# A cross network in one-and-a-half levels of Winograd products: two tiles side by side, a third inner product, residual sums by DMA

## The chip, the cores and the metric

The kernel runs on one core of a Trainium2 chip. A core has five engines, each with an instruction queue that it works off in order: TensorE (PE) multiplies, VectorE (DVE) and ScalarE (ACT) work elementwise, GpSimd (POOL) and SyncE (SP) here mostly issue transfers. They wait for each other by semaphores. Operands lie in SBUF, 128 partitions wide; products land in PSUM, eight banks of 128 x 512 float32. Sixteen DMA engines move data between HBM and SBUF.

The metric is the device time of one execution in microseconds, the median over runs.

## The reference

A deep cross network with L = 6 layers on B = 16384 tokens of D = 1024 features, in bfloat16:

```
x = x0
for l in range(6):
    proj = einsum('bd,de->be', x, ws[l]) + bs[l]     # 16384 x 1024 times 1024 x 1024
    x = x0 * proj + x
return x
```

The work is six 1024 x 1024 matrix products for every token, and beside each a bias, a product with `x0` and a residual sum.

## The kernel before, in words

**Tiles.** Activations are held transposed: features on partitions, tokens along the free dimension. A tile (`pair`, `pr`) has 1024 tokens; there are 16. A *unit* is one layer of one tile; there are 96, in the order tile 0 layers 0 to 5, tile 1 layers 0 to 5, and so on (`units`). `x0T` holds the tile's input, `xst` its running x, each in two buffers that the tiles take in turn; each is cut in four blocks by feature half and token half: B11, B12, B21, B22 (`blk`).

**Seven products instead of eight.** A unit is a 2 x 2 block product by Winograd's variant of Strassen's method. Four sums of input blocks (T1 to T4, VectorE) and four sums of weight blocks (named 5, 6, 7, 3) allow seven block products: P1, P2, P5, P6, P3, P7, P4. Each is 512 x 512 weights on 512 tokens: four groups (`group`, line 286) of four matmuls of 512 columns, every group into one PSUM bank. The groups of P1, P6, P7 and P4 go into banks `pA`, those of P2, P5, P3 into banks `pX`. ScalarE empties the banks: `biased` (line 296) adds the layer's bias and writes one of the SBUF tiles `ev` (P1s, P5s, Q, U, V, W), `copy` (line 293) copies without bias, F.m from `pA` to `pX` so that P3 accumulates on P6's partial sum. VectorE then adds P5's part (Ua, Va) and P1's (Q1), multiplies by `x0` (Qm, Um, Vm, Wma, Wmb) and adds the old x (Qa, Ux, Vx, Wx). All these elementwise operations go through `tt` (line 202).

**A second level inside two products.** In most units products 5 and 2 are themselves split into seven (`inner`, line 398): 28 matmuls of 256 columns in place of 16 of 512. That needs three more VectorE operations ahead (t13, t2, t4), seven copies on ScalarE (e_p5, f1, e_c11, f2, e_c12, e_u3, e_c21) and one more sum on VectorE (cc) for each such product, and inner weight sums (5i, 2i). The first tile's six units and the last unit are one-level (`level1`): there 112 matmuls of 512 columns; elsewhere 80 of 512 and 56 of 256.

**Weights.** The first tile's units load the raw weight blocks, make the sums 5, 6, 7, 3 and the inner sums on VectorE (`combo`, `icombo`) and save these to HBM (`Lc`, `save`, line 306, issued by GpSimd). Later units load everything, nine tiles of 512 KB, into a ring of 16 (`ring_seq`, `pump`, line 250, SP's queue). A tile is reloaded as soon as its last use has been emitted.

**Order of the work.** Every operation carries a rank, written by hand or found before and kept as text (`R2`, `R0`, `EARLY`, `RLAST`): a time within its unit. A heap emits the operations whose predecessors are emitted in the order of unit start plus rank; each engine's queue has the order that results. On SP's queue weight loads stand between the transposing loads of the next tile's `x0` (`ld`, line 533), the transposes of finished tiles (`tro`, line 538) and their stores (`sto`, line 544).

**The last unit** is one-level and has its own end: its parts are transposed by DMA and on TensorE and stored in pieces.

Of the kernel before, what the change touches and what calls it, by code (L numbers as in the profile page):

```python
# [16 lines left out]

def ranks(text):

    return {w.split("@")[0]: float(w.split("@")[1]) for w in text.split()}  # L20

R2 = ranks("""
P1.0@0 P1.2@0.86 5p5@1.73 5p1@2.16 P1.3@2.6 2p1@3.46 5p2@3.9 5p6@4.34 2p5@4.78 P1.1@5.21 5p7@6.08 5p3@6.51 2p2@6.95
2p6@7.39 5p4@7.82 P6.0@8.26 P6.1@9.13 2p7@9.99 2p3@10.43 P3.0@10.86 2p4@11.73 P6.2@12.16 P6.3@13.03 P3.1@13.89
P3.2@14.75 P3.3@15.62 P7.1@16.48 P7.0@17.34 P7.2@18.21 P7.3@19.07 P4.1@19.93 P4.0@20.8 P4.2@21.66 P4.3@22.52
E1.0@1.07 5e_p5@2.38 5f1@3.03 E1.2@3.48 5e_c11@4.55 5f2@5.2 2e_p5@5.65 2f1@6.3 5e_u3@6.75 E1.3@7.23 2e_c11@7.8 E1.1@8.28  # L30
2f2@8.85 5e_c21@9.33 F.0@9.81 5e_c12@10.43 2e_u3@10.9 2e_c12@11.38 F.1@11.86 2e_c21@12.37 E3.0@12.85
F.2@13.45 F.3@14.1 E3.1@14.96 E3.2@15.82 E3.3@16.69 E7.0@18.41 E7.1@18.98 E7.2@19.55 E7.3@20.14 E4.0@21.87 E4.1@22.44
E4.2@23.01 E4.3@23.59
T1@-1.14 5t13@0.59 5t2@3.06 2t13@3.39 5t4@5.13 2t2@6.6 T2@6.93 2t4@8.07 T4@8.4 T3@9.6 5cc@10.88 2cc@12.61 Q1@13.35
Qm@14.62 Qa@15.89 Ua@17.43 Um@18.7 Ux@19.97 Va@21.11 Wma@23.38 Wmb@24.58 Wx@25.31 Vm@27.38 Vx@28.85
""")
R0 = ranks("""
P1.0@0 P1.1@.9 P1.2@1.7 P1.3@2.6 P2.2@3.5 P2.3@4.4 P2.1@5.2 P2.0@6.1 P5.2@6.9 P5.1@7.8 P5.0@8.7 P5.3@9.5
P6.2@10.4 P6.0@11.3 P6.1@12.1 P6.3@13 P7.2@13.9 P3.2@14.7 P7.1@15.6 P3.1@16.4 P3.0@17.3 P7.0@18.2 P3.3@19 P7.3@19.9
P4.0@20.8 P4.2@21.6 P4.1@22.5 P4.3@23.3  # L40
F1.2@2.8 F1.0@3.2 F1.3@3.7 F1.1@4.1 E2.2@4.6 E2.1@6.3 E2.0@7.2 E2.3@7.7 E5.2@8.3 F.2@11.5 E5.1@11.9 E5.3@12.4
F.1@13.2 E5.0@13.6 E7.2@14.9 E3.2@15.8 F.0@16.4 E7.1@16.8 F.3@17.4 E3.1@17.8 E7.0@19.2 E3.0@19.8 E3.3@20.4
E7.3@21 E4.0@21.8 E4.2@22.7 E4.1@23.6 E4.3@24.4
Qm@14.5 Qa@18.6 Ua@21.1 Um@22.4 Va@23.5 Wma@25.2 Wmb@25.3 Wx@26.4 Ux@27.6 T1@4.6 Vm@30 Vx@31.2 T2@8.3 T3@9.8 T4@13
c5@-8.6 c6@-6.8 c7@-4.5 c3@11.9 2i7@-7.4 2i5@-7.1 2i6@.5 2i3@9.4 5i5@10.9 5i7@11.2 5i6@11.6 5i3@14.2
""")
SAVES = ranks("gate@15 s5@16 s6@17 s7@18 s3@20 s2i@21 s5i@22")
EARLY = [ranks("""
t0.0@-4.00 u0.0@-3.70 t0.1@-3.80 u0.1@-3.50 t0.2@-3.60 u0.2@-3.30 t0.3@-3.40 u0.3@-3.10
t1.0@-1.90 u1.0@-1.60 t1.1@-1.70 u1.1@-1.40 t1.2@-1.50 u1.2@-1.20 t1.3@-1.30 u1.3@-1.00  # L50
t2.0@.3 t2.1@.4 t2.2@2.1 t2.3@2.2 u2.0@.5 u2.1@.6 u2.2@2.2 u2.3@2.3
P1.1@-2.83 bT@-2.4 P1.0@-1.96 P1.2@-1.10 P1.3@-.24 P2.1@1.27 P2.0@3.3 P2.2@4.49 P2.3@5.35 P5.1@6.94 P5.0@7.81 P5.3@8.67
P5.2@9.53 P6.3@10.52 P6.2@11.38 P6.0@12.24 P7.3@13.11 P6.1@13.97 P7.0@14.83 P4.3@15.70 P7.2@16.56 P7.1@17.42
P4.0@18.29 P4.2@19.15 P4.1@20.01 P3.0@20.88 P3.1@21.74 P3.3@22.60 P3.2@23.47
F1.1@-.9 F1.0@-.8 F1.2@2.25 F1.3@2.35 E2.1@2.7 E2.0@4.60 E2.2@5.56 E2.3@6.42 E5.3@9.74 E5.0@10.22 F.3@11.59
E5.2@12.07 E5.1@12.54 F.0@13.31 E7.3@14.18 F.2@14.75 F.1@15.23 E7.0@15.90 E4.3@16.77 E7.2@17.63 E7.1@18.49 E4.2@20.22
E4.0@20.79 E4.1@21.36 E3.0@21.95 E3.1@22.81 E3.3@23.67 E3.2@24.54
T1@3.57 c5@5.67 c5b@5.8 c6@5.9 T2@9.25 2i5@9.3 2i7@9.4 2i6@9.5 c7@10.38 T3@11.52 T4@12.65 2i3@13.79 c3@14.12
Qm@15.26 5i5@17.53 Va@19.74 Qa@20.88 Vm@22.01 Wma@23.15 Wmb@23.75 Wx@24.49 Ua@25.63 Um@26.90 Ux@28.17 5i7@29.30
Vx@30.77 5i6@31.91 5i3@41.53  # L60
"""), ranks("""
P1.3@.13 P1.2@.99 P1.0@1.86 P1.1@2.72 P2.2@3.58 P2.3@4.45 P2.0@5.31 P2.1@6.17 P5.3@7.04 P5.2@7.90 P5.1@8.76 P5.0@9.62
P6.3@10.49 P6.1@11.35 P6.2@12.21 P7.3@13.08 P6.0@13.94 P7.2@14.80 P4.3@15.67 P7.0@16.53 P7.1@17.39 P4.2@18.26
P3.3@19.12 P4.0@19.98 P4.1@20.85 P3.0@21.71 P3.1@22.57 P3.2@23.44
F1.2@2.06 F1.3@2.54 F1.0@3.02 F1.1@3.79 E2.3@5.52 E2.2@6.09 E2.1@7.24 E2.0@7.81 E5.3@8.38 E5.1@9.83 F.3@11.56
E5.2@12.04 F.1@12.51 E5.0@12.99 F.2@13.47 E7.3@14.15 F.0@15.01 E7.2@15.87 E7.0@17.60 E7.1@18.46 E4.3@19.03 E4.2@19.61
E3.3@20.19 E4.1@21.92 E4.0@22.49 E3.0@23.06 E3.1@23.64 E3.2@24.51
c5@-7.81 2i5@-5.93 c6@-5.59 T1@5.44 5i5@8.04 T2@8.38 2i6@9.51 c7@9.85 2i3@10.98 T3@11.32 5i6@12.45 T4@12.79 c3@13.92
Qm@15.06 2i7@17.00 Qa@17.67 Va@19.21 Wmb@20.35 Vm@20.95 Wma@23.23 Wx@23.97 Ua@25.25 5i7@26.39 Um@26.72 Ux@27.99
Vx@30.40 5i3@33.80  # L70
"""), ranks("""
# [77 lines left out]
def kernel(  # L149
# [13 lines left out]
    H = D // 2  # L163
    NB = 512
    PR = 2 * NB
    assert D == 1024 and B % PR == 0
    NPAIR = B // PR
    KQ, HQ, NQ = KH // 2, H // 2, NB // 2
    RING = 16
# [475 lines left out]
```

## Time and profile before

| | us |
|---|---|
| median of 3 runs | 2270.79 (2270.66 to 2271.06) |
| profiled execution, span | 2269.4 |
| TensorE busy | 2248.5 |
| VectorE busy | 2092.1 |
| ScalarE busy | 1847.8 |
| GpSimd busy | 24.5 |
| a steady two-level unit | 23.38 |

| DMA | |
|---|---|
| moved | 557.02 MB, mean 245 GB/s |
| SP's queue, share of 16 engines' time | 78.6% |
| GpSimd's queue | 2.3% |
| landing of a weight tile of 512 KB, median | 4.7 us (saved sums), 5.2 us (raw weights) |
| landing of a transpose, median | 7.3 us |
| landing of an output store of 1 MB, median | 8.8 us |

The profiled execution's own time is the span from its first to its last instruction, 2269.4 us; the median of the runs stands 1.4 us above it. The busy time of an engine is the union of its instructions' times. Instructions of one engine overlap, so how much room one takes is read from the distance of the starts of neighbours and not from its duration: a matmul of 512 columns lasts 379 ns and the next starts 216 ns after it.

### The profile page before, as it was taken

The numbers are of one execution on the slowest core, as the hardware profiler recorded it, in microseconds if no ns is written. First come the engines' busy times: TensorE is split into PE (matmuls) and PEld (weight loads), VectorE is DVE, ScalarE is ACT, GpSimd is POOL, SyncE is SP. The second block draws the span as 40 slices with busy tenths as digits, with TensorE's granted clock in tenths as the row PEclk, the third lists the DMA queues.
The fourth block names the chain that finished last, engine by engine and source line by source line (L and its number), as shares of the span: only waits on it lengthen the run. The fifth ranks groups of instructions, "written<-read, shape, count | busy, mean of one in ns | idle before, by whom it ended". The sixth has DMA issues, their size and how long they took to land.

```text
span 2269.4 us, 34750 instructions
## 1 busy us (share of the span) xinstructions
PE 2248.5 (99%) x12754; PEld 1267.4 (56%) x12993; DVE 2092.1 (92%) x2331; ACT 1847.8 (81%) x3234; POOL 24.5 (1%) x46
## 2 busy tenths in 40 slices
PE   9999999999999999999999999999999999999998
PEld 4455555555555555555555555555555555555554
DVE  8999999999999999999999999999999999999997
ACT  6678888888888888888888888888888888888887
POOL 1110000000000000000000000000000000000000
PEclk9999999999999999999999999999999999999999
DMA  8779797796977969779697796977969689696872
GB/s 279 229 270 301 251 249 264 220 303 206 251 259 224 288 220 248 264 218 288 215 266 251 227 285 205 277 242 227 288 201 294 225 225 294 195 295 224 236 247 66
DMA packets 620492, 557.02 MB, mean 245 GB/s; under 512 B 391456, under 2 KB 546592, under 8 KB 620320
## 3 DMA queue, kind: packets, MB, share of 16 engines
q1 hardware_dynamic: 614240, 534.58, 78.6%
q0 software_dynamic: 5488, 19.93, 2.3%
q8 instruction: 102, 1.67, 0.3%
q14 instruction: 70, 0.57, 0.1%
q10 hardware_dynamic: 592, 0.27, 0.0%
HBM read 437.79 MB, written 52.43 MB: 216 GB/s over the span
## 4 chain that ended last, share of the span: by engine, by line
PE 99%; issue 1%; DMA 0%; ACT 0%; SPq 0%; DVE 0%; ACTq 0%
PE pA L289 58%; PE pX L411 24%; PE pX L289 17%; DMA ev<-in_x_dram 0%; ACT pX L294 0%; PE pA L505 0%; PE pX L359 0%; PE pX L505 0%; DVE x0T L516 0%; ACT ev L294 0%; ACT x0T L363 0%; ACT ip L294 0%; SPq L577 0%; SPq L574 0%; ACTq L294 0%
## 5 line engine op out<-in xcount | busy, mean ns | idle before, releaser
L289 PEld LDWEIGHTS <-wp 128*128 128x128 bf16 x7904 | 772.9, 98 | 838.1 <-issue 0.9
L289 PE MATMUL pA<-T,wp 128*128 128x512 bf16 x4468 | 1033.0, 379 | 7.3
L298 ACT ACTIVATE ev<-pA,b_all 128x512 bf16<-128x512 f32 x1123 | 717.5, 692 | 211.2 <-PE pA L289 164.0
L411 PEld LDWEIGHTS <-wp 128*128 128x128 bf16 x4984 | 487.7, 98 | 151.5 <-issue 0.2
L202 DVE TENSOR_TENSOR ev<-ev,x0T 128x2048 bf16<-128x2048 bf16 (+2 forms) x483 | 483.0, 1002 | 8.1 <-ACT ev L298 1.5
L202 DVE TENSOR_TENSOR ev<-ev,ev 128x2048 bf16<-128x2048 bf16 (+1 forms) x283 | 343.9, 1216 | 71.7 <-ACT ev L298 44.6
L202 DVE TENSOR_TENSOR xst<-ev,xst 128x2048 bf16<-128x2048 bf16 x319 | 389.1, 1220 | 19.1 <-PE pX L289 0.9
L411 PE MATMUL pX<-ti,wp 128*128 128x256 bf16 x2848 | 397.8, 273 | 0.0
L298 ACT ACTIVATE ev<-pX,b_all 128x512 bf16<-128x512 f32 x412 | 285.4, 697 | 63.8 <-PE pX L289 62.9
L289 PE MATMUL pX<-xst,wp 128*128 128x512 bf16 x1371 | 323.3, 379 | 0.3
L289 PE MATMUL pA<-xst,wp 128*128 128x512 bf16 x1205 | 302.4, 379 | 3.9
L294 ACT CAST ev<-pX 128x512 bf16<-128x512 f32 x384 | 232.1, 606 | 47.9 <-ACT ev L298 37.4
L294 ACT COPY pX<-pA 128x512 f32<-128x512 f32 x412 | 237.5, 602 | 21.7 <-PE pA L289 18.7
L294 ACT COPY pX<-pX 128x512 f32<-128x512 f32 x356 | 207.8, 584 | 8.6 <-ACT ip L294 0.2
L202 DVE TENSOR_TENSOR T<-xst 128x2048 bf16<-128x2048 bf16 x160 | 195.0, 1218 | 0.3
L202 DVE TENSOR_TENSOR T<-xst,T 128x2048 bf16<-128x2048 bf16 x160 | 195.0, 1219 | 0.2
L294 ACT CAST iu<-pX 128x512 bf16<-128x512 f32 x356 | 192.7, 601 | 0.0
L202 DVE TENSOR_TENSOR ev<-iu,ip 128x1024 bf16<-128x1024 bf16 x178 | 123.2, 692 | 60.7 <-ACT iu L294 60.7
L411 PE MATMUL pX<-T,wp 128*128 128x256 bf16 x1068 | 160.2, 273 | 0.0
L294 ACT CAST ip<-pX 128x512 bf16<-128x512 f32 x178 | 104.7, 589 | 54.0 <-PE pX L411 54.0
L411 PE MATMUL pX<-xst,wp 128*128 128x256 bf16 x888 | 133.2, 273 | 0.1
L202 DVE TENSOR_TENSOR xst<-ev,x0T 128x2048 bf16<-128x2048 bf16 x64 | 78.3, 1223 | 1.6
(50 smaller groups left out, 636.4 us busy)
## 6 DMA issues: line engine op xcount, KB each, us to landing
wp<-Lc SPq DMA_DIRECT2D x538, 512.0 KB, 4.7
wp<-in_ws_dram SPq DMA_DIRECT2D x287, 512.0 KB, 5.2
out_dram<-x0T SPq DMA_DIRECT2D x30, 1024.0 KB, 8.8
Lc<-wp POOLq DMA_DIRECT2D x24, 512.0 KB, 6.1
Lc<-isum POOLq DMA_DIRECT2D x12, 512.0 KB, 6.8
w<-in_ws_dram SPq DMA_DIRECT2D x5, 512.0 KB, 6.1
ev<-in_x_dram SPq DMA_DIRECT2D x3, 512.0 KB, 7.2
out_dram<-x0T SPq DMA_DIRECT2D x3, 256.0 KB, 4.2
```

The costliest lines, as they stand in the source:

```text
L202: nc.vector.tensor_tensor(out=o, in0=a, in1=b, op=op)
L289: nc.tensor.matmul(bank[:], lhsT=wt[(u, w)][:, k, m * P:(m + 1) * P], rhs=rhs[:, k, :], start=(start and k == 0), stop=(k == KH - 1), skip ...
L294: add(name, lambda: nc.scalar.copy(out=dst, in_=src), rd, wr)
L298: add(name, lambda: nc.scalar.activation(out=dst, in_=src, func=IDENT, bias=b_all[:, c:c + 1], scale=1.0), rd, wr)
L411: nc.tensor.matmul(pX[bank][:, m * NQ:(m + 1) * NQ], lhsT=wv[:, k, m * P:(m + 1) * P], rhs=rhs[:, k, :], start=(start and m == 0 and k == ...
```

## The change

1. *Order of units.* Tiles are taken in groups of two. The two (lanes) alternate by layer: layer 0 of the one, layer 0 of the other, layer 1 of the one, and so on. `x0T` gets a third buffer, `xst` one per lane, and a buffer `stage` takes the transposed output, which was written over `x0T` before. In the first group `stage` also holds the inner weight sums.
2. *Weights are shared.* The two units of a layer use the same loaded tiles: ten tiles (with the new 3i) per layer and group instead of nine per unit. The ring has 12 tiles instead of 16, and the separate pool for the raw block `w12` is gone.
3. *A third product in two levels.* Product 3 gets t13, t2, t4, 28 matmuls of 256 columns, seven copies and cc like 5 and 2. It no longer accumulates on P6 (the copies F go); E6 empties P6 with the bias into U, and a new VectorE sum Ub adds product 3 (tile C3). The sums u0 and u1 of the inner products stay in the product's own tile, where cc adds in place. The first tile's six units and the last unit stay one-level.
4. *Residual.* In layer 0 the bias carries +1 (`b_all`), so that x0 * (proj + 1) is the new x and the four additions go. In layers 1 to 5 the blocks Q and U are added to x by an accumulating DMA from GpSimd's queue, SBUF to SBUF; V and W stay with VectorE. Wma and Wmb become one operation.
5. *Order of operations.* The rank tables go. TensorE's order is written out as lists (`PE_FIRST`, `PE_ONE`, `PE_TWO`, `PE_LAST`); the other queues are ordered by a list scheduler (`schedule`) that plays through the program with a duration and a latency for each operation, and takes on each engine, of those ready, the one whose result is due first. Due times are worked back from TensorE's order.

```diff
+PE_TWO = """
+5p5 5p1 P1.1 P1.0 2p5 5p2 2p1 5p6 P1.3 P1.2 5p3 2p2 5p7 2p6 P6.0 5p4 2p3 3p5 2p7 3p1 P6.1 2p4 3p2 P6.2 3p6 P6.3 P7.0
+P7.1 3p3 P7.3 3p7 P7.2 P4.0 3p4 P4.1 P4.3 P4.2
+""".split()
...
+def schedule(ops):
...
+    late = [0.0] * n
+    for i in range(n - 1, -1, -1):
+        if i in nominal:
+            late[i] = nominal[i]
+        else:
+            late[i] = min([late[j] for j in succ[i]] + [ops[i].due]) - ops[i].lat
...
+        while future[e] and future[e][0][0] <= s:
+            i = heapq.heappop(future[e])[1]
+            heapq.heappush(now[e], (late[i], i))
+        i = heapq.heappop(now[e])[1]
+        order.append(i)
+        start[i] = s
+        free[e] = s + ops[i].occ
...
-    RING = 16
+    RING = 12
     NDUMMY = 8
+    INNER = "523"
...
-    x0Ts = [work.tile([P, 2, KD, NB], BF16, name=f"x0T{i}") for i in range(2)]
+    x0Ts = [work.tile([P, 2, KD, NB], BF16, name=f"x0T{i}") for i in range(3)]
     xsts = [work.tile([P, 2, KD, NB], BF16, name=f"xst{i}") for i in range(2)]
+    stage = work.tile([P, 2, KD, NB], BF16, name="stage")
...
-    units = [(pr, l) for pr in range(NPAIR) for l in range(L)]
+    units = [(2 * g + s, l) for g in range(NGROUP) for l in range(L) for s in range(2)]
...
+    plain = lambda u: (units[u][0] == 0) or u == NU - 1
...
+            ring_seq += [(gl, w, "load") for w in "1 5 5i 2 2i 6 3 3i 7 4".split()]
...
+        def pe(name, occ, fn, rd, wr, weights=(), u=u, gl=gl, line=line, at=0.0):
+            op(f"{name}@{u}", "PE", occ, occ + 0.19, fn, rd, wr, [(gl, w) for w in weights], key=(u, line[name]), at=at)
...
+        def act(name, fn, rd, wr, biased_=False, u=u, occ=None):
+            occ = occ or (0.571 if biased_ else 0.475)
+            op(f"{name}@{u}", "ACT", occ, occ + 0.17, fn, rd, wr)
...
+        def dve(name, fn, n, rd, wr, weights=(), u=u, gl=gl, at=0.0, due=FAR):
+            occ = n / 1920 + 0.068
+            op(f"{name}@{u}", "DVE", occ, occ + 0.12, fn, rd, wr, [(gl, w) for w in weights], at=at, due=due)
...
+        if u == 1:
+            for n in range(2):
+                def ld(n=n, pr=pr, x0T=x0T):
+                    nc.sync.dma_start_transpose(out=x0T[:, n], in_=x0[pr * PR + n * NB:pr * PR + (n + 1) * NB, :])
+                op(f"ld{n}@{u}", "SP", 5.0, 9.0, ld, [], [X0[0, n], X0[1, n]], at=17.0)
...
+                nc.vector.tensor_scalar_add(b_all[:, 0:KD], pA[KH - 1][:, 0:KD], 1.0)
+                nc.vector.tensor_copy(out=b_all[:, KD:LK], in_=pA[KH - 1][:, KD:LK])
...
-            for X, Bm, src, a, b, C in (("5", T[1][:], "T1", 0, 1, P5s), ("2", B21, XI[1, 0], 2, 3, Q)):
+            for X, a, b in (("5", 0, 1), ("2", 2, 3), ("3", 0, 1)):
...
+            if one:
+                copy(f"F.{m}", pX[m][:], pA[m][:], [A[m]], [Xn[m]])
+                group(f"P3.{m}", "3", pX[m], Xn[m], B22, [XI[1, 1], Xn[m]], m, False)
+                biased(f"E3.{m}", U[:, m, :], pX[m][:], 0, m, [Xn[m]], [f"U.{m}"])
+            else:
+                biased(f"E6.{m}", U[:, m, :], pA[m][:], 0, m, [A[m]], [f"U.{m}"])
...
+            if not one:
+                ttop("Ub", U[:], U[:], C3[:], ADD, allm("U") + allm("3c"), allm("U"))
...
+                if l == 0:
+                    ttop(nm + "m", blk(xst, *q), C[:], blk(x0T, *q), MULT, allm(nm) + [X0[q]], [XO[q]])
+                    continue
+                ttop(nm + "m", C[:], C[:], blk(x0T, *q), MULT, allm(nm) + [X0[q]], allm(nm))
+                if nm in "QU":
+                    def acc(C=C, q=q, xst=xst):
+                        nc.gpsimd.dma_start(blk(xst, *q), C[:], accum_op=ADD)
+                    op(f"{nm}x@{u}", "POOL", 1.0, 9.5, acc, allm(nm) + [XO[q]], [XO[q]])
...
+                    ttop(nm + "x", blk(xst, *q), C[:], blk(xst, *q), ADD, allm(nm) + [XO[q]], [XO[q]])
...
+        for pt in ([pr - 1, pr] if not last else [pr - 1]) if l == L - 1 and lane == 1 else []:
+            ot, xt = (pt % 2, xsts[pt % 2])
             for n in range(2):
...
+                op(f"tro{n}.{ot}@{u}", "SP", 5.0, 9.0, tro, [f"xs.{ot}.0{n}", f"xs.{ot}.1{n}"], STG[n])
...
+                op(f"sto{n}.{ot}@{u}", "SP", 1.0, 10.0, sto, STG[n], ())
```

## The prediction

> **What bounds the kernel now.** I read the page first: the span, the busy shares and the chain of work that ended last.
>
> ```profile
> span 2269.4 us, 34750 instructions
> ...
> PE 2248.5 (99%) x12754; PEld 1267.4 (56%) x12993; DVE 2092.1 (92%) x2331; ACT 1847.8 (81%) x3234; POOL 24.5 (1%) x46
> ...
> PE 99%; issue 1%; DMA 0%; ACT 0%; SPq 0%; DVE 0%; ACTq 0%
> ```
>
> TensorE is busy 99% of the span and the ending chain runs through it alone: time falls only if TensorE gets less to do, and only while the others keep up. VectorE, at 92%, has the least room. Next, the table by stretches of the span (engine busy time with instruction counts, granted clock, DMA share, GB/s): one stretch of the first pair, then two of one steady layer each.
>
> ```profile
> 82.00:106.00 24.00, 23.84 (x110) 10.88 (x112) 23.63 (x29) 16.19 (x29) 2.66 (x5) 1.00 1.06 293
> ...
> 1070.20:1093.60 23.40, 23.24 (x135) 13.34 (x137) 21.68 (x25) 19.38 (x35) 0.00 (x0) 1.00 0.60 203
> 1093.60:1117.00 23.40, 23.30 (x136) 13.31 (x137) 21.68 (x25) 19.38 (x35) 0.00 (x0) 1.00 0.63 203
> ```
>
> A steady layer repeats every 23.38 us (the same 33-matmul piece of the chain starts at 990.08 and, two layers on, at 1036.84). VectorE is busy 21.68 us of it and idle 1.70; the clock is full. The first row matters later: there VectorE was busy 23.63 of 24 us and TensorE still had no gap. Then the timeline of TensorE (start, duration, operation), for the pitch of the two sizes of matmul:
>
> ```profile
> 1003.33 0.60 PE L411 MATMUL pX<-T,wp 128*128 128x256 bf16 x4
> 1003.77 0.60 PE L411 MATMUL pX<-x0T,wp 128*128 128x256 bf16 x4
> 1004.20 1.04 PE L411 MATMUL pX<-ti,wp 128*128 128x256 bf16 x8
> ...
> 1010.70 2.75 PE L289 MATMUL pX<-x0T,wp 128*128 128x512 bf16 x12
> 1013.29 7.07 PE L289 MATMUL pA<-T,wp 128*128 128x512 bf16 x31
> ```
>
> Starts, not durations, give the pitch, since matmuls overlap: 2.59 us for twelve 512-column matmuls is 0.2158 each; four 256-column ones take 0.437, 0.1092 each. Check: 80 x 0.2158 + 56 x 0.1092 = 23.38, the whole layer without a gap. The timeline of VectorE gives its pitches:
>
> ```profile
> 1003.45 0.42 DVE L202 TENSOR_TENSOR ti<-x0T,ti 128x512 bf16<-128x512 bf16 x1
> 1003.78 1.22 DVE L202 TENSOR_TENSOR T<-x0T,T 128x2048 bf16<-128x2048 bf16 x1
> ...
> 1009.97 1.23 DVE L202 TENSOR_TENSOR ev<-ev,ev 128x2048 bf16<-128x2048 bf16 x1 [0.31 <-ACT ev L294]
> 1011.23 1.22 DVE L202 TENSOR_TENSOR ev<-ev,x0T 128x2048 bf16<-128x2048 bf16 x1
> ...
> 1019.01 1.22 DVE L202 TENSOR_TENSOR T<-xst 128x2048 bf16<-128x2048 bf16 x1
> 1020.14 0.69 DVE L202 TENSOR_TENSOR ev<-ev,x0T 128x1024 bf16<-128x1024 bf16 x1
> 1020.75 0.68 DVE L202 TENSOR_TENSOR ti<-T 128x1024 bf16<-128x1024 bf16 x1
> ```
>
> So 1.13 us for 2048 elements (1.26 when it needs the result just before it), 0.60 for 1024, 0.33 for 512. Last, GpSimd's timeline and the DMA issues (count, size, median landing), nearest to the new accumulating DMA:
>
> ```profile
> 33.79 2.29 POOL L306 DMA_DIRECT2D Lc<-wp  x4
> ...
> wp<-Lc SPq DMA_DIRECT2D x538, 512.0 KB, 4.7
> ...
> Lc<-wp POOLq DMA_DIRECT2D x24, 512.0 KB, 6.1
> Lc<-isum POOLq DMA_DIRECT2D x12, 512.0 KB, 6.8
> ```
>
> **The change, part by part.** A unit is one layer of one 1024-token tile; there are 96. Seven stay one-level in both kernels (the first tile's six and the last unit), 89 are two-level.
>
> *Third product in two levels.* In each of the 89 units, 16 matmuls of 512 columns become 28 of 256: 16 x 0.2158 - 28 x 0.1092 = 0.395 us. 89 x 0.395 = 35.2 us off TensorE, which is the path. A two-level unit becomes 22.99 us.
>
> *VectorE.* Before, a two-level unit has 14 operations of 2048, 6 of 1024, 4 of 512: 15.82 + 3.60 + 1.32 = 20.7; measured busy is 21.68, so about 0.9 us goes on results needed at once (seven times 0.13). After, for layers 1 to 5: t13, t2, t4 and cc of product 3 come (0.60 + 2 x 0.33 + 0.60), the sum Ub comes (1.13), Qa and Ux go (-2.26), and the two halves of Wm become one (-0.07): +0.66, so 22.3 us. In layer 0 the bias carries +1 and all four additions go (two beyond those, -2.26): 20.1. The mean is (5 x 22.3 + 20.1)/6 = 22.0 us of 22.99, or 96%. In the first group the one-level unit, which also makes the weight sums, has 16 of 2048 and 12 of 512: 22.0 + 0.9 of its 24.2 us. It lies beside TensorE; at nothing, as long as it is never late. For that speaks the stretch at 82 to 106 us. The alternation helps too: a tile's next layer starts one whole unit (23 us) after its last product, where before it started at once.
>
> *ScalarE.* Casts and copies end at a pitch of 0.48 (1002.02 to 1002.50), biased evictions at 0.58. Seven copies of product 3 replace four F copies, E6 replaces E3: +3 x 0.48 on 19.38 gives 20.8 us, 91%. Hidden by TensorE; if that cover goes, each late eviction holds a PSUM bank and so a matmul.
>
> *Accumulating DMAs.* Two per unit in layers 1 to 5, 512 KB, SBUF into SBUF, issued by GpSimd. An issue there took 0.57 us (four in 2.29) while VectorE was busy without a break, so GpSimd has room. No trace row shows an accumulation. Its landing is bounded below by the quickest plain GpSimd transfer of this size, 3.0 us, and above by the longest, 12.7, plus a second read. A steady layer moves nine weight tiles at a DMA share of 0.62: 0.62 x 23.4 / 9 = 1.6 us of all engines each, so the second read is put at 1.6 and the top at 14.3. I take 6.8 + 1.6 = 8.4, from the row that also starts in SBUF; the planner in the change assumes 9.5.
> What waits for it: the next tile's E6.0 writes U, which the DMA still reads. In the new TensorE order 3p4 ends 2.59 us before the unit's end (20.4). Copy, cc, Ub and Um take 0.8 + 0.7 + 1.25 + 1.25, so Um ends 1.4 us into the next unit. P7.0 begins after eight one-level groups and eighteen inner ones (8 x 0.863 + 18 x 0.437 = 14.8) and needs E6.0 (0.7) done. So landings up to 14.1 - 1.4 = 12.7 us cost nothing, if ScalarE's queue doesn't stop earlier: E6.0 may stand in line ahead of 3f1 and the last copies of products 2 and 3, and their matmuls wait for those. Q's transfer has more room.
> The Trainium skill, "SBUF — State Buffer", section "SBUF: two separate sides", speaks against this part: descriptors of a GpSimd DMA can starve while VectorE holds the shared port, one sentence there giving about 620 ns alone against 3100 beside a copy. By that rule each accumulation would start some 2.5 us later (an estimate from that page), which 12.7 us would still hold, so the sum is the same. The row above, 0.57 us per issue beside a full VectorE, shows no starving.
>
> *Weights shared.* Ten tiles per two units instead of nine per unit: 5 x 1.6 = 8 us of DMA per unit instead of 14.5, and the accumulations return about 2 x 3.2. Worth nothing in time, since no TensorE wait before is on a steady weight load. The ring shrinks from 16 to 12: tile 5i gets its slot after P1.2 of the second unit (6.1 us) and is wanted 16.9 us later, against 4.7 to land, leaving 12.2 us. That holds unless transposes, about 5 us of SP's queue each, stand ahead: the two tiles' output (four) and the next x0 (two of four) now meet at one end of a group. Six in a row would be 30 us. Weight issues are emitted between them, so I take 0 and keep 0 to 2 us at each of 7 boundaries and some 2 more in group 0.
>
> *Start and end.* Pair 1's x0 is now wanted at 34 us, not at 155; two transposes issued at 17 us occupy SP for 9.8 us (as at 1031.86) and land near 30, then T1 and 5t13 follow (1.7). VectorE is full then (19.82 of 20 us from 14 to 34). Bounds 0 and 6, taken 1. At the end pair 14 must still be transposed and stored during the last unit: accumulation (8), transpose (7.3 and one behind it), store (8.8) come to about 30 us after unit 94, against 24.2 + 6 for unit 95: 0 to 6, taken 1. I see no gain in either.
>
> *List scheduler.* It replaces fixed ranks by a plan made of the same pitches (0.863, 0.436, 1.13). TensorE's order stays a written list. It costs nothing at run time; a misordered queue would show as one of the rivals.
>
> Sum: 2269.4 - 35.2 + 2 = 2236.2 profiled; the median of the runs stands 1.4 above the profiled span, so 2237.6, say 2238.
>
> **The rivals.**
> - *VectorE becomes the bound* (slower). If the 1.70 us of idle waits per unit stay on top of 22.0, a unit takes 23.7, 89 x 0.7 = 62 us more: 2300. It decides once waits exceed 1.4 us a unit. For it: layers 1 to 5 leave 0.7 us. Against: the waits before are VectorE waiting for evictions with nothing else ready; a second tile gives it other work.
> - *The accumulation is late* (slower). Each us beyond the slack costs 74 us (two-level units of layers 1 to 5); half a us eats the gain. At 1 us over: 2310; at 3, 2460. For it: saves landed as late as 12.7. Against: those were issued in batches of up to seven, and the DMA engines now have less weight traffic.
> - *Gaps at the ends of groups* (a smaller gain): 7 x 2 to 4 us for transposes ahead of weights, or 0.2 us a unit from PSUM banks evicted late: 2252 to 2266.
> - *The stalls eat it all*: 0.4 us a unit, 2271.
>
> **How the numbers follow.** Forecast 60%, its own range 2231 to 2248; smaller gain 13%; no change 4%; late accumulation 13%; VectorE bound 10%. Faster is 73%, same 4%, slower 23%; 0.2% (4.5 us) is about what a measurement of this kernel tells from none. To leave out no more than 2 in 10, the range runs from 2231 through the smaller gains up to the VectorE case, 2300.
>
> **What would show it.** Right: 6480 weight loads of the one-level kind and 7476 of the inner kind; a steady pair of units every 46.0 us with TensorE gapless; VectorE 94 to 97%, ScalarE about 90%; accumulations landing in 7 to 10 us; no ScalarE wait on one. Wrong: TensorE waiting on ScalarE copies behind an E6 that waits for a DMA; VectorE at 99% with TensorE idle behind T or t13; weight waits every 276 us.

## The result and the profile after

The changed kernel takes 2437.5 us (median of 4 runs, 2428.2 to 2446.0), the kernel before 2270.7 beside it (4 runs, 2270.4 to 2271.1): a ratio of 1.073, with a 95% interval of 1.071 to 1.076. The prediction said 2238 us and a range up to 2300. It is 200 us off, with the wrong sign.

The page of the changed kernel: span, busy shares, TensorE's busy tenths and granted clock by slices, GpSimd's DMA queue (packets, MB, share of 16 engines' time), the chain that ended last.

```profile
span 2444.2 us, 37883 instructions
...
PE 2260.5 (92%) x14061; PEld 1378.5 (56%) x14061; DVE 2083.1 (85%) x2484; ACT 1992.9 (82%) x3501; POOL 164.1 (7%) x210
...
PE   8999999898797998979979799897998979979997
...
PEclk9999999999898999989989999998999989999998
...
q0 software_dynamic: 29104, 105.92, 22.0%
...
PE 76%; DMA 11%; DVE 7%; SPq 3%; issue 2%; ACT 0%; POOL 0%; POOLq 0%; DVEq 0%; ACTq 0%
```

TensorE is down from 99% to 92% of a longer span, the chain now has 11% of DMA waits in it, and no other engine is near its limit: VectorE stands at 85%. The dips in TensorE's row, 7 and 8 among nines, come two per group of two tiles, and the clock dips with them. So time is lost in places, not spread over all units. The list of waits (us in total, times, longest) names them:

```profile
ACT ev L295 <- DMA xst<-ev: 110.7, 10, 17.6
DVE T L181 <- DMA xst<-ev: 97.3, 6, 17.7
...
PE pA L282 <- ACT ev L295: 82.8, 6, 15.3
...
PEld L282 <- DMA wp<-Lc: 59.4, 7, 14.9
PE pA L282 <- DMA wp<-Lc: 56.2, 7, 14.6
```

Ten times ScalarE's evictions with bias and six times VectorE's sums wait, up to 17.7 us, for an accumulating DMA (`xst<-ev`), and TensorE waits six times, 82.8 us in all, for those evictions. Seven times TensorE waits up to 14.6 us for a weight tile. The timeline (start, duration, operation, idle time before it) shows a quiet stretch and then one event of each kind; line 301 is the transposing load of the next x0, 479 the accumulation, 566 the transposing of finished tiles, 295 an eviction, 282 and 425 matmuls:

```profile
1017.36 0.60 PE L425 MATMUL pX<-ti,wp 128*128 128x256 bf16 x4
1040.34 0.60 PE L425 MATMUL pX<-ti,wp 128*128 128x256 bf16 x4
...
1063.91 30.74 SPq L301 DMA_TRANSPOSE x0T<-in_x_dram  x2
...
1066.30 0.86 POOL L479 DMA_DIRECT2D xst<-ev  x1 [5.90 <-ACT ev L295]
...
1092.06 1.26 ACT L295 ACTIVATE ev<-pA,b_all 128x512 bf16<-128x512 f32 x2 [16.87 <-DMA xst<-ev]
...
1092.80 3.57 PE L282 MATMUL pA<-T,wp 128*128 128x512 bf16 x8 [14.54 <-ACT ev L295]
...
1097.97 1.89 PE L282 MATMUL pA<-T,wp 128*128 128x512 bf16 x8
...
1217.90 21.69 SPq L566 DMA_TRANSPOSE stage<-xst  x2
...
1244.33 3.59 PE L282 MATMUL pA<-T,wp 128*128 128x512 bf16 x8 [11.72 <-DMA wp<-Lc]
```

The first two lines are the same place of two successive units: 22.98 us apart, as predicted (23.38 before), with no gap between. Then two transposes occupy SP's queue for 30.74 us, where two took 9.84 in the kernel before:

```profile
1031.86 9.84 SPq L533 DMA_TRANSPOSE x0T<-in_x_dram  x2
```

The accumulation issued 2.4 us after they began lands some 25 us later, and ScalarE, VectorE and TensorE stand still for it. At 1217.90 two other transposes, also beside an accumulation, hold SP's queue for 21.69 us, and the weight loads behind them come 11.72 us late. In the table by stretches (busy time of each engine, then granted clock, DMA share, GB/s) the first event looks like this:

```profile
1065.00:1070.00 5.00, 5.00 (x36) 3.29 (x34) 5.00 (x5) 4.65 (x9) 0.86 (x1) 1.00 1.13 290
...
1075.00:1080.00 5.00, 3.25 (x21) 1.95 (x20) 0.10 (x1) 0.19 (x1) 0.00 (x0) 1.00 1.34 64
1080.00:1085.00 5.00, 0.00 (x0) 0.00 (x0) 0.00 (x0) 0.00 (x0) 0.00 (x0) 0.77 1.22 59
```

The DMA engines are shown as full (1.22 to 1.34) while they move 59 to 64 GB/s instead of 290.

**Where 208 us went**, against the 2236.2 that the working gave for the profiled run. I summed TensorE's gaps over 0.3 us: 166.0 us in 27 of them. Six mid-group ones of 10.4 to 15.3 us make 82.8; those at group ends about 74; one at 35.7 us is the start (5.8). After a gap the granted clock is one half for a while: 173.7 us of the span in all, 95.9 of it within gaps and 13.3 behind the last matmul, where it costs nothing; the other 64.5, at half speed, cost some 32.3 (eight matmuls took 3.57 us at 1092.80 and 1.89 at 1097.97). From the last matmul to the end there are 16.3 us, before 6.1. With the 35.2 us saved, 2269.4 - 35.2 + 166.0 + 32.3 + 10.2 = 2442.7, against 2444.2 measured.

The Trainium skill, "TensorE: Matmul & The Clock Gate", Part 1, says that the array's clock falls to half after about 3.4 us of idleness and returns after about as long a stretch of work. The run agrees roughly: full clock returned near 1096.3, 3.5 us after the matmul at 1092.80, and 2.6 to 5.9 us after the others of these gaps. It fell 2.2 to 5.0 us into them, so that a gap of 2.5 us, at 1278.4, was already long enough once.

### The profile page after: what moved, and what is told of

Read it like the earlier page. It is cut to its first block, busy times and chain, and to the rows that moved or that the text cites. A ratio compares the mean times of both kernels' runs of the same rounds, so it can differ in the third digit from the quotient of the medians.

```text
span 2444.2 us, 37883 instructions
## 1 busy us (share of the span) xinstructions
PE 2260.5 (92%) x14061; PEld 1378.5 (56%) x14061; DVE 2083.1 (85%) x2484; ACT 1992.9 (82%) x3501; POOL 164.1 (7%) x210
## 4 chain that ended last, share of the span: by engine, by line
PE 76%; DMA 11%; DVE 7%; SPq 3%; issue 2%; ACT 0%; POOL 0%; POOLq 0%; DVEq 0%; ACTq 0%
PE pA L282 46%; PE pX L425 28%; DMA xst<-ev 6%; DMA wp<-Lc 4%; DVE ev L181 4%; PE pX L282 2%; SPq L566 2%; DVE T L181 1%; DVE ti L181 1%; DMA wp<-in_ws_dram 0%; DVE xst L181 0%; SPq L306 0%; ACT ev L295 0%; SPq L592 0%; DMA x0T<-x0T 0%
## 5 line engine op out<-in xcount | busy, mean ns | idle before, releaser
L282 PE MATMUL pA<-T,wp 128*128 128x512 bf16 x4608 | 1125.0, 385 | 139.0 <-ACT ev L295 82.8
L295 ACT ACTIVATE ev<-pA,b_all 128x512 bf16<-128x512 f32 x1479 | 998.9, 693 | 290.7 <-PE pA L282 138.7
L425 PEld LDWEIGHTS <-wp 128*128 128x128 bf16 x7188 | 705.5, 98 | 273.6 <-DMA wp<-Lc 23.8
L291 ACT CAST ev<-pX 128x512 bf16<-128x512 f32 x1096 | 612.2, 593 | 78.8 <-PE pX L425 59.6
L425 PE MATMUL pX<-ti,wp 128*128 128x256 bf16 x4056 | 585.0, 274 | 18.4 <-DMA wp<-Lc 18.4
L181 DVE TENSOR_TENSOR ev<-ev,ev 128x2048 bf16<-128x2048 bf16 x372 | 449.0, 1213 | 14.7 <-ACT ev L295 9.4
L181 DVE TENSOR_TENSOR ev<-ev,x0T 128x2048 bf16<-128x2048 bf16 (+1 forms) x324 | 387.4, 1203 | 0.8 <-ACT ev L295 0.5
L479 POOL DMA_DIRECT2D xst<-ev x158 | 135.4, 857 | 2105.1 <-ACT ev L291 1052.9
L425 PE MATMUL pX<-xst,wp 128*128 128x256 bf16 x1736 | 261.7, 273 | 0.0
L181 DVE TENSOR_TENSOR xst<-ev,xst 128x2048 bf16<-128x2048 bf16 x158 | 192.8, 1220 | 2.5
L181 DVE TENSOR_TENSOR ev<-ev,ip 128x1024 bf16<-128x1024 bf16 x267 | 182.7, 684 | 4.1 <-ACT ev L291 4.0
L181 DVE TENSOR_TENSOR ti<-xst,ti 128x512 bf16<-128x512 bf16 x296 | 124.1, 420 | 27.4 <-PE pX L425 24.6
## 6 DMA issues: line engine op xcount, KB each, us to landing
out_dram<-stage SPq DMA_DIRECT2D x30, 1024.0 KB, 10.2
```

The source lines that it names most:

```text
L181: nc.vector.tensor_tensor(out=o, in0=a, in1=b, op=op)
L282: nc.tensor.matmul(bank[:], lhsT=wt[(gl, w)][:, k, m * P:(m + 1) * P], rhs=rhs[:, k, :], start=(start and k == 0), stop=(k == KH - 1), ski ...
L291: act(name, lambda: nc.scalar.copy(out=dst, in_=src), rd, wr)
L295: act(name, lambda: nc.scalar.activation(out=dst, in_=src, func=IDENT, bias=b_all[:, c:c + 1], scale=1.0), rd, wr, True)
L425: nc.tensor.matmul(pX[bank][:, m * NQ:(m + 1) * NQ], lhsT=wv[:, k, m * P:(m + 1) * P], rhs=rhs[:, k, :], start=(start and m == 0 and k == ...
L479: nc.gpsimd.dma_start(blk(xst, *q), C[:], accum_op=ADD)
```

## The experiments

Theories at the start. **C**, collision: a transfer of GpSimd's queue and a DMA transpose in flight together slow each other down (C1: only the accumulating one does this; C2: any transfer of GpSimd's queue). **S**: the ring of 12 tiles and SP's crowded queue make weights late at group ends by themselves. **A**: an accumulation is simply slow. All times are beside the kernel before at 2270.6 to 2271.0. Where no interval is given, the time is that of one run; the four runs of the changed kernel lie within 18 us.

### Without the accumulations

```diff
-                    def acc(C=C, q=q, xst=xst):
-                        nc.gpsimd.dma_start(blk(xst, *q), C[:], accum_op=ADD)
-                    op(f"{nm}x@{u}", "POOL", 1.0, 9.5, acc, allm(nm) + [XO[q]], [XO[q]])
+                    pass
```

> The changed kernel with the accumulating DMAs left out, nothing in their place: in layers 1 to 5 the blocks Q and U of x stay as layer 0 left them. Theory C (an accumulating DMA and a transposing DMA in flight together slow each other several times over, and every gap of TensorE goes back to that, directly or through weight loads that stand behind the slow transposes on SP's queue): the gaps in the middle of a group (10 to 15 us) and those at its end (4 to 15 us) both go, two transposes take about 10 us of SP again, the granted clock is 1.000, 2236 to 2246 us. Theory S (the ring of 12 tiles and the many transposes on SP's queue make weights late at the ends of groups by themselves): only the gaps in mid-group go; 74 us of gaps and some 18 us of half clock stay, about 2330 us. Theory A (an accumulation is simply slow): as theory C.

2266.1 us, 20 above the range that C gave. The gaps fall from 166 to 18 us and the transposes take 4.0 to 8.2 us. What is left: weights late by 1 to 3 us at group ends (S is real and small), and a tail of 12.3 us.

### Plain copies in place of accumulations

```diff
-                        nc.gpsimd.dma_start(blk(xst, *q), C[:], accum_op=ADD)
+                        nc.gpsimd.dma_start(blk(xst, *q), C[:])
```

> The changed kernel with each accumulating DMA replaced by a plain copy of the same 512 KB, same source, same destination, same GpSimd queue: the residual sum of the blocks Q and U is left out in layers 1 to 5. Theory C1 (the accumulation is what collides with transposes): no long gaps, 2236 to 2250 us, transposes at 5 to 7 us each. Theory C2 (any transfer of GpSimd's queue collides with transposes): transposes still 10 to 30 us for two, 2350 to 2440 us. Theory S: about 2330 us. Theory A: 2236 to 2250 us.

2349.4 us, just under C2's range. Gaps 76.9 us; the copies land in 3.5 us at the median, yet six times ScalarE waits up to 11.1 us for one. The durations of the transposes by tile (ns: min/median/max) reach 13.2 us:

```profile
L301 SPq DMA_TRANSPOSE x0T<-in_x_dram x28: 4789/7364/13212, 106.6 to 2027.5; - x28
...
L566 SPq DMA_TRANSPOSE stage<-xst x30: 4772/6764/10552, 289.3 to 2319.1; - x30
```

In the kernel, then, C1 alone is wrong: a plain copy on the same queue collides as well. With the addition the loss against the kernel without any such transfer is about twice as large (171 us against 83).

### Without transposes

```diff
-                    nc.sync.dma_start_transpose(out=x0T[:, n], in_=x0[pr * PR + n * NB:pr * PR + (n + 1) * NB, :])
+                    nc.sync.dma_start(x0T[:, n].rearrange("p k b -> p (k b)"),
+                                      x0[pr * PR + n * NB:pr * PR + (n + 1) * NB, :].rearrange("(p j) d -> p (j d)", p=P))
...
-                    nc.sync.dma_start_transpose(out=stage[:, n]..., in_=xst[:, n]...)
+                    nc.sync.dma_start(stage[:, n]..., xst[:, n]...)
```

> The changed kernel with the transposing loads of x0 (all but the first tile's) and the transposes of finished tiles replaced by plain transfers of the same 1 MB on the same queue: the data is not transposed. The accumulations stay. Theory C: accumulations land in 5 to 8 us throughout, no gap over 3 us, 2236 to 2250 us. Theory S: the gaps at the ends of groups stay as far as stores hold SP's queue, 2260 to 2330 us. Theory A: as the changed kernel, 2430 us, with accumulations landing as late as 26 us.

2247.9 us, with every accumulation in place. Gaps 3.3 us in all; no wait on an accumulation is longer than 1.8 us (the list of waits: us in total, times, longest):

```profile
ACT ev L295 <- DMA xst<-ev: 9.9, 8, 1.7
DVE T L181 <- DMA xst<-ev: 9.1, 6, 1.8
```

The last matmul ends at 2232.3. The accumulations land in 5.8 us at the median and 12.1 at most, where C had said 5 to 8. A falls: without transposes the change does what it was predicted to do. The ring of 12 tiles by itself falls as well; what the transposes cost by holding SP's queue this run doesn't tell, since it takes them off that queue. The run without accumulations tells it: 1 to 3 us at a group's end.

### The two kinds of transfer alone and together

Ten phases between barriers, each made of these calls:

```python
def turn_in():
    for n in range(2):
        nc.sync.dma_start_transpose(out=x0T[:, n], in_=x0[n * NB:(n + 1) * NB, :])
def accum(k=2):
    for i in range(k):
        nc.gpsimd.dma_start(acc[i][:], ev[:], accum_op=ADD)
```

> No network at all: ten phases one after the other on an otherwise idle core, and a copy of x0 to the output. Two 1 MB transposes from HBM alone; two accumulations of 512 KB alone; both together; two 1 MB transposes within SBUF alone; these with two accumulations; two plain copies on GpSimd's queue alone; these with two transposes; four weight loads alone; these with two accumulations; four weight loads with two transposes. Theory C1: the two mixed phases of accumulation and transpose take 25 to 35 us each, against 10 and 6 to 9 us alone, the others at most the sum of their parts (plain copies with transposes 13 to 16 us, weights with accumulations 10 to 14 us). Theory C2: plain copies with transposes also take over 20 us. Theory A: the accumulations alone take over 15 us, and mixing adds nothing beyond the sum.

GpSimd's timeline: a one-element copy marks each landing (`x0T`: transposes, `acc`: accumulations).

```profile
21.34 0.19 POOL L65 COPY tok<-x0T 128x1 bf16<-128x1 bf16 x1 [4.16 <-DMA x0T<-in_x_dram]
22.17 1.90 POOL L53 DMA_DIRECT2D acc<-ev  x2 [0.64 <-SPq L66]
...
29.56 0.19 POOL L65 COPY tok<-acc 128x1 bf16<-128x1 bf16 x1 [2.33 <-DMA acc<-ev]
30.33 1.74 POOL L53 DMA_DIRECT2D acc<-ev  x2 [0.59 <-SPq L66]
...
56.65 0.19 POOL L65 COPY tok<-x0T 128x1 bf16<-128x1 bf16 x1 [3.38 <-DMA x0T<-in_x_dram]
```

Two transposes alone take 10.7 us (10.62 to 21.34), two accumulations alone 7.4 (22.17 to 29.56), both together 26.3 (30.33 to 56.65): longer than one after the other, 18.1. A single accumulation alone lands in 4.75 us, here in 9.1 and 22.1. With transposes from SBUF it is 23.6 against 19.1. Weight loads lose nothing beside accumulations (14.5 against 16.0), nor transposes beside weight loads on ScalarE's queue (16.2 against 19.3), nor two plain copies beside transposes (13.8 against 15.1). In these phases, then, only accumulations collide, as C1 has it, while plain copies did in the kernel. VectorE is idle in all of them, so the collision doesn't need a busy VectorE.

### VectorE makes all the additions

```diff
-                if nm in "QU":
+                if False:
```

> All the residual additions by VectorE again, none by the accumulating DMA; the computation is whole. If the collision of accumulations with transposes is what costs (C), the long gaps before P7.0 and half of the group-end gaps go, but VectorE now has 2 x 1.2 us more per unit in layers 1 to 5: 22.3 + 2.3 = 24.6 us there against 20.1 in layer 0, a mean of 23.85 us per unit over 90 units against TensorE's 22.98, if nothing carries over from layer 0 to the others: 2310 to 2330 us with the ends; where layer 0's spare time is carried over, 2290. The one without any additions stood at 2266, so it can't be much below 2266. If instead the time was lost to anything else that the accumulations do not cause, it stays above 2400.

2285.3 us, a little under the 2290 expected at best. TensorE's gaps are 24.8 us, most of them weights late by up to 4 us at group ends; no gap behind VectorE is longer than 2.6 us, though that is now busy 97% of the span.

### Only the loads of the next x0 moved

```diff
-        if u >= 2 and l == 0:
+        if l == L - 1 and lane == 0 and grp + 1 < NGROUP:
+            pn, x1 = pr + 2, xsts[1]
+            op(f"pin@{u}", "POOL", ..., nc.gpsimd.tensor_copy(xn[:, :, 0, 0:1], x1[...]), ...)
+            load_next(pn, [f"pin@{u}"])
+        if u >= 2 and l == 0 and lane == 1:
+            load_next(pr, [])
```

(`load_next` issues a tile's two transposing loads; `pin` is a small copy by GpSimd that reads x and writes the x0 buffer, so that the loads behind it wait for the accumulations of layer 4)

> The accumulations stay as they are in every layer; only lane 0's two transposing loads of the next group's x0 are moved, from the unit in which they meet the accumulations of layer 5 to the one before, in hardware order behind the accumulations of layer 4. If the collision makes the mid-group gaps (82.8 us and the clock after them), those six gaps of 10 to 15 us go and the ones at the group ends stay: 2444 less some 100 to 120 us, so 2320 to 2345. If the gaps come from what layer 5's or layer 0's unit does to the accumulation whatever the loads do, they stay: 2430 to 2450.

2344.7 us, just inside the range for C. The mid-group gaps go, those at the group ends stay: there two transposes of finished tiles beside accumulations of layer 5 still take 21.63 us:

```profile
1166.57 21.63 SPq L580 DMA_TRANSPOSE stage<-xst  x2
```

### Accumulations and transposes kept apart

```diff
-                if nm in "QU":
+                if nm in "QU" and l < L - 1:
```

(on top of the moved loads)

> As the one with the moved loads, and besides layer 5's two additions are made by VectorE, so that no accumulation is in flight while the transposing stores at the group's end read x. The computation is whole. If the collision is the cause of both kinds of gaps (C), none above 5 us stays, and it stands with the kernel without accumulations, or a little below, since the transposes are no longer slowed: 2245 to 2270 us. VectorE has 2.3 us more in the 14 units of layer 5, 24.6 us, of which layer 0's 20.1 us beside it takes up most. If only one kind goes, 2320 to 2360. If neither, 2400 or more.

2303.9 us, ratio 1.014 (1.012 to 1.016): 41 us better again, but 34 above the top of the range. No wait of ScalarE or VectorE on an accumulation is left among the long ones; six gaps of 4.4 to 8.0 us at group ends are weights up to 8.4 us late. On SP's queue the moved loads and the four transposes of finished tiles stood nearly one behind the other. So S, small without accumulations, grows with the order on that queue.

### Which queue it is: phases

> Nine isolated phases between barriers, nothing of the kernel's computation (the output is a copy of x0): (1) two transposes from HBM alone; (2) two 512 KB copies within SBUF on ScalarE's queue alone, (3) with the transposes; (4) four weight loads on GpSimd's queue alone, (5) with the transposes; (6) four 512 KB saves to HBM on GpSimd's queue alone, (7) with the transposes; (8) one accumulation with the transposes; (9) transposes issued first and two accumulations after them. If it is GpSimd's queue as such that collides with transposes, (5) and (7) take longer than the two parts in sequence, and (3) does not. If it is reading and writing SBUF by accumulation (C1), (3), (5) and (7) take no more than the sum (17, 19, 19 us), (8) takes 3 to 6 us more than 10.7 + 4.8 - 2, and (9) is as bad as the 26.3 us that accumulations first took. If it is any transfer within SBUF, (3) is above its sum.

Transposes alone took 10.2 us, then with copies on ScalarE's queue 13.8 (sum 14.5), with four saves of GpSimd's 15.2 (sum 17), with one accumulation 14.8 (sum 15), with four weight loads of GpSimd's queue 21.8 (sum 19.1; each transpose landed in some 18 us), before two accumulations 21.9 (sum 17.6). Weight loads, then, collide too once they come by GpSimd's queue, while four of them by ScalarE's queue had lost nothing (16.2 us); the small pieces of work lose nothing in total. Of the two signs named for GpSimd's queue as such, the one with weight loads came, the one with saves did not. The phase with the weight loads on GpSimd's timeline (the transposes begin at 49.54):

```profile
49.97 2.98 POOL L69 DMA_DIRECT2D wp<-in_ws_dram  x4 [0.60 <-SPq L77]
...
71.33 0.19 POOL L73 COPY tok<-x0T 128x1 bf16<-128x1 bf16 x1 [2.77 <-DMA x0T<-in_x_dram]
```

### Weights on GpSimd's queue

```diff
-            nc.sync.dma_start(t[:], w_src(gl % L, w))
+            (nc.sync if gl < L else nc.gpsimd).dma_start(t[:], w_src(gl % L, w))
```

(on top of all additions by VectorE)

> VectorE makes all residual additions (2285 us so), and the weights of all groups after the first are loaded by GpSimd's queue instead of SP's, where they stood behind the transposes; the computation is whole. If what is left of the loss at the group ends comes from SP's queue holding the weights (S), the seven gaps of 2 to 4 us and the half clock behind them go: 24.8 + 20 less some 5 for the two ends, so 2245 to 2255 us. If transposes slow any transfer of GpSimd's queue, weights included, the gaps grow to what accumulations showed, 10 us and more per group: 2350 or above. If VectorE is behind the gaps, it stays at 2285.

2425.1 us, the outcome named for the case that weights collide too, 140 more than with the same loads on SP's queue. There is no accumulation in this kernel and no transfer within SBUF but the transposes, and those reach 25.5 and 32.6 us (ns: min/median/max):

```profile
L301 SPq DMA_TRANSPOSE x0T<-in_x_dram x28: 3725/9023/25467, 153.7 to 2093.0; - x28
...
L566 SPq DMA_TRANSPOSE stage<-xst x30: 4790/5478/32617, 309.4 to 2395.1; - x30
```

With the weights on SP's queue the longest were 8.6 and 9.5 us:

```profile
L301 SPq DMA_TRANSPOSE x0T<-in_x_dram x28: 4057/5610/8557, 154.8 to 1973.3; - x28
...
L566 SPq DMA_TRANSPOSE stage<-xst x30: 4796/5858/9539, 292.1 to 2255.1; - x30
```

The weights themselves are late by 5.6 us at most; VectorE waits up to 27.1 us for a transpose to have read x, and ScalarE and TensorE wait behind it:

```profile
DVE xst L181 <- DMA stage<-xst: 131.9, 9, 27.1
```

For C2 this is a strong run: same loads, same tiles, another queue. It doesn't tell GpSimd's queue from any other second queue, since on SP's queue the loads stand in line with the transposes and are not beside them. The phases do (21.8 us against 16.2 by ScalarE's queue), and the copies on ScalarE's queue below.

### The last stores on GpSimd's queue too

```diff
-                        nc.sync.dma_start(out[...], stage[...])
+                        (nc.gpsimd if last else nc.sync).dma_start(out[...], stage[...])
```

(on top of the weights on GpSimd's queue)

> As the one with weights on GpSimd's queue, and the stores of the last group's first tile (the tail of 16 to 19 us against 6 before) go by GpSimd's queue too, so that the last tile's three stores on SP do not stand behind them. Expected 3 to 8 us under the other, 2238 to 2250, a ratio to before of 0.985 to 0.992, if S holds; no gain over it if the tail is the time that the transfers take and not their order on the queue.

2438.3 us, ratio 1.076 (1.073 to 1.079), its runs between 2421 and 2457: nothing gained over the one before. The tail, from the last matmul to the end, is 24.6 us against 18.7, and what was said of S could not be seen under the collision.

### Plain copies on ScalarE's queue

```diff
-                        nc.gpsimd.dma_start(blk(xst, *q), C[:], accum_op=ADD)
+                        nc.scalar.dma_start(blk(xst, *q), C[:])
-                    op(f"{nm}x@{u}", "POOL", 1.0, 9.5, acc, allm(nm) + [XO[q]], [XO[q]])
+                    op(f"{nm}x@{u}", "ACT", 0.7, 9.5, acc, allm(nm) + [XO[q]], [XO[q]])
```

> The two accumulations are plain copies within SBUF as in the kernel with plain copies (2349 us; the residual is not added), but issued on ScalarE's queue instead of GpSimd's. If it is GpSimd's queue that collides with the transposes, the long gaps go and the transposes land in 6 to 10 us: ScalarE has 2 x 0.6 to 0.7 us more per unit, 20.8 + 1.3 = 22.1 us against 22.98, so 2250 to 2290 us, with any more only from ScalarE waiting for VectorE's products. If it is the transfer within SBUF whatever its queue, 2330 to 2360, with transposes of 15 us and more as on GpSimd's queue.

2302.3 us, 47 less than on GpSimd's queue and 12 above the range. The longest transposes are 8.8 and 9.2 us, against 13.2 and 10.6:

```profile
L301 SPq DMA_TRANSPOSE x0T<-in_x_dram x28: 4791/6610/8818, 106.1 to 1983.0; - x28
...
L566 SPq DMA_TRANSPOSE stage<-xst x30: 4792/6534/9198, 287.5 to 2272.7; - x30
```

No wait on a copy remains among the long ones. Of the gaps left at group ends (six of 3.8 to 5.6 us) four end with a late weight and two, of 4.2 us each, with VectorE's sum `ti`. The kernel still stands 36 us above the one without any such transfer (2266.1): copies on ScalarE's queue do less harm, but they are not free.

The Trainium skill, "DMA: Bandwidth & Descriptors", section "Queues, rings and completion order", says that a DMA engine goes round the queues that have work, packet by packet. That alone would make a copy on ScalarE's queue disturb a transpose as much as one on GpSimd's. Here the queue makes a difference of 47 us, so the measurement goes beyond the rule. Why GpSimd's queue is different, and why isolated copies and saves on it lose nothing, no run here shows.

### A version that beats both

```diff
-        for pt in ([pr - 1, pr] if not last else [pr - 1]) if l == L - 1 and lane == 1 else []:
...
+        if l == 0 and grp > 0:
+            turn(pr - 2, 0, [f"P4.2@{u - 1}"])
+            turn(pr - 2, 1, [f"tro0.{lane}@{u}"])
...
-                op(f"ld{n}@{u}", "SP", 5.0, 9.0, ld, [], [X0[0, n], X0[1, n]], after=gate)
+                op(f"ld{n}@{u}", "SP", 5.0, 9.0, ld, [], [X0[0, n], X0[1, n]],
+                   after=[f"P4.2@{u - 2}"] if lane == 1 and n == 1 else gate)
```

(on top of all additions by VectorE; `turn` holds the old transpose and store of one half tile, which now come in the next group's layer 0, where few weight slots come free, instead of all at the end of layer 5)

> VectorE makes all residual additions (2285 us so), all DMA on the queues as before the change, and the group's four transposing stores and the second transposing load of lane 1's next x0 are moved on SP's queue behind the weight loads of layer 5 and spread over the first unit of the next group, where no weight slots come free. The computation is whole. If the loss left at the group ends is weight loads that stand behind transposes on SP's queue (S), most of the 24.8 us of gaps and the 10 to 15 us of half clock behind them go: 2245 to 2262 us, a ratio to before of 0.989 to 0.996. If the transposes only meet other loads there, 2275 to 2290.

2263.3 us (5 runs, 2261.7 to 2263.7), ratio to before 0.9965 (0.9951 to 0.9979), a gain of 0.35%, just above the range. Its page:

```profile
span 2261.6 us, 37125 instructions
...
PE 2216.9 (98%) x13795; PEld 1372.6 (61%) x14061; DVE 2216.8 (98%) x2642; ACT 2000.0 (88%) x3501; POOL 28.4 (1%) x52
...
PE   8999999999999999999999999999999999999996
...
PE 85%; DVE 11%; issue 2%; SPq 1%; ACT 1%; DMA 1%; POOLq 0%; POOL 0%; ACTq 0%
```

TensorE's row is even again, no wait on a steady weight load is left, and the gaps over 0.3 us sum to 9.8 us. Most units take 22.98 us; twelve of those behind the first group, read from the starts of their weight loads, take 23.1 to 23.8, where VectorE (98% busy, 11% of the chain) holds TensorE. Loads that stood behind transposes were the rest of S. What keeps it from 2238: those units (6.9 us together), the gaps at the start (4.4) and one of 2.7 near the end with 1.7 us of half clock behind it, and 18.9 us after the last matmul, against 6.1 before.

### Is the tail an order?

```diff
-            op(f"sto{n}.{ot}@{u}", "SP", 1.0, 10.0, sto, STG[n], ())
+            op(f"sto{n}.{ot}@{u}", "SP", 1.0, 10.0, sto, STG[n], (), due=NU * 22.95 - 25.0 if last else FAR)
```

(on top of the spread transposes)

> As the kernel with spread transposes (2263.3 us, 19 us from the last matmul to the end of the span), with a due time 25 us before the end for the two stores of the last group's first tile, so that VectorE finishes that tile's residual sooner and its transposes and stores go ahead of the last tile's on SP's queue; the computation is whole. If the tail of 16 to 19 us against 6 before is that order, the end comes 5 to 12 us earlier: 2251 to 2258 us, a ratio to before of 0.991 to 0.995. If it is the time that the last 2 to 3 MB take whatever their order, 2261 to 2265.

2273.4 us, ratio 1.001 (1.000 to 1.002). The tail is 16.9 us instead of 18.9, so the order is worth about 2 us. But at 2164 and 2170 TensorE waits 2.9 and 8.2 us for VectorE's sums `ti`, where the kernel without the due time has one gap of 2.7, and that costs more; it fits a changed order in VectorE's queue, which is argued here and not shown. Whether the rest of the tail is transfer time alone stays open.

## Why the prediction was wrong

- **Third product, 35.2 us off TensorE: right.** The steady unit is 22.98 us against 22.99 predicted, with the 6480 and 7476 weight loads foretold (7188 and, from `stage` in the first group, 288), and without transposes the whole kernel ran in 2247.9.
- **VectorE hidden, its rival at 2300: right.** VectorE was 85% busy in the changed kernel and 93% without transposes, where nothing stretched the span; the mean of the working comes to 21.9 us a unit and not 22.0, and measured are 21.7. With all additions back on it, it kept up at 97 to 98%; with the transposes spread, twelve units were late by up to 0.8 us. So the accumulating DMA relieved an engine that hardly needed it; the prediction never priced the kernel without it.
- **Accumulating DMA, taken 8.4 us and bounded at 14.3: the step that failed.** The quiet case was over-estimated (4.75 us alone, 5.8 at the median) and the top was too low: 26.5 us in the kernel. The bounds came from rows of plain transfers, to which a second read was added; none asked what else was in flight. Nor was the slowing of the *other* transfer counted: the transposes beside it went from 9.84 to 30.74 us a pair.
- **A possible warning stood in the profile of before.** Its timeline has two transposes that took 18.59 us in the first tile, next to GpSimd's saves, where the later pairs took 9.4 to 12.1:

```profile
72.64 0.53 POOL L306 DMA_DIRECT2D Lc<-wp  x1 [1.61 <-DVE wp L202]
...
73.17 18.59 SPq L533 DMA_TRANSPOSE x0T<-in_x_dram  x2
...
74.11 0.53 POOL L306 DMA_DIRECT2D Lc<-isum  x1 [0.94 <-DVE isum L202]
```

  The change puts GpSimd transfers beside transposes in every group. That this outlier was the same collision is not shown: the DMA engines moved 258 to 375 GB/s there and not 59 to 64, and four saves beside two transposes lost nothing in the phases (15.2 us against 17).
- **The rival "accumulation late": right mechanism, wrong count.** The chain was the one named: E6.0 held by the DMA, P7.0 behind it. But it was priced as some us in each of 74 units; it was 10 to 15 us in six, wherever transposes were in flight, and the slack of 12.7 us did hold elsewhere. The weights behind slow transposes belong to another rival, "gaps at the ends of groups", priced at 7 x 2 to 4 us, where they came to about 74.
- **Weights, 0 to 2 us at each of 7 boundaries: nearly right without accumulations (1 to 3 us), wrong with them (up to 14.6).** The condition was named, "unless transposes stand ahead", but a transpose was priced at 5 us of SP's queue where it took about 11 in the collision.
- **Start and end, taken 1 us each:** 5.8 us of gap at the start, inside the 0 to 6 kept; 10.2 us more at the end, beyond its 6. The end is mis-sized in the repaired kernels too.
- **Not in the working at all:** the half clock behind the gaps of some us, 32.3 us.
- The rule of the Trainium skill's "SBUF — State Buffer", section "SBUF: two separate sides", weighed against this part, was not what cost the time: an accumulation's issue took 0.86 us beside a busy VectorE, far from the 2.5 us of extra delay that the estimate from it gave, and the collision showed in the phases with VectorE idle.

## What to carry to other kernels

Before work is moved to another DMA queue, list which transfers will be in flight beside it, and look in the trace for any place where those two kinds already meet; an outlier there (18.59 us among pairs of 9.4 to 12.1) asks a question that the medians don't. A transfer's price in a quiet row is no upper bound when it can slow others: count what stands behind those too, and the half clock that follows each gap. And price the change without its riskiest part: here the same kernel with the additions left on VectorE and the transposes spread was the one that gained.

## What the runs showed of the hardware

- **Accumulating transfers of GpSimd's queue and DMA transposes in flight together** take longer than one after the other: 26.3 us for what takes 10.7 and 7.4 alone. In the kernel the engines are shown as full there at 59 to 64 GB/s. In the kernels it happened with plain copies of that queue too (transposes to 13.2 us), and the longest transposes were those beside a stream of weight loads from HBM (32.6 us); the same copies on ScalarE's queue and the same loads on SP's left the transposes at 8.6 to 9.5 us at most. A few isolated copies or saves lost nothing in total.
- **An accumulating transfer** of 512 KB within SBUF lands in 4.75 us alone, against 2.9 for a plain one; its packets of 4 KB take 334 ns at the median in the changed kernel, against 159 in the kernel with plain copies, and its issue 0.86 us against 0.53.
- **TensorE's clock** fell to half 2.2 to 5.0 us into gaps of 2.5 to 15.3 us and stayed there for 2.6 to 5.9 us of work (3.5 after the gap that ends at 1092.80).
